# Attention of a fused attention and expert kernel: heads in groups of four instead of two, the softmax sums of the first block as matrix products

## The chip, the core and the metric

The kernel runs on one core of a Trainium2 chip. Four engines of that core matter here: TensorE (PE in the rows; PEld is its weight load), VectorE (DVE), ScalarE (ACT) and GpSimd (POOL), each with an instruction queue that it works through in order; SP issues most DMAs. Matrix products end in PSUM, eight banks of 512 fp32 columns on 128 partitions; everything else lives in SBUF. The metric is the device time in microseconds (us), the median of the runs shown.

## The reference, cut to what matters

```python
def _attn_ref(q, k, v, cap):                 # q, k, v: 4 x 12 x 448 x 64
    scores = scale * np.matmul(q, k.transpose(0, 1, 3, 2))
    scores = cap * np.tanh(scores / cap)     # cap = 30
    scores = scores - np.max(scores, axis=-1, keepdims=True)
    attn = np.exp(scores)
    attn = attn / (np.sum(attn, axis=-1, keepdims=True) + 1e-09)
    return np.matmul(attn, v)
def _moe_ref(x, w_in, w_out, s, b):          # x: 1792 x 768, d_ff 2048
    r = np.maximum(x @ w_in, 0.0)
    return (s * (r * r) + b) @ w_out
def _moe2_ref(x, phi, w1, w2):               # 8 experts with 4 slots each
    logits = x @ phi
    d = softmax of the logits over tokens; slot_input = d.T @ x
    slot_out = relu(slot_input @ w1) @ w2    # per expert
    return (softmax of the logits over slots) @ slot_out
```

The attention's output (12 heads of 64, side by side) is `x` of the second function, whose result is `x` of the third.

## The kernel before

The four batch entries are four blocks of 448 tokens. A block's attention covers 12 heads, taken in six pairs; its result `x` (768 rows of features on six times 128 partitions, 448 tokens wide, kept as a rounded part and a remainder) is the moving operand of the hidden layer (`hidden`, L373), 16 column groups of 18 products `hp` each.

A pair's attention goes in `STEPS` = 8 steps of the generator `attention` (L188). Its 448 keys are four chunks of 112. At steps 0, 2, 4 and 6 `scores` (L104) makes one chunk for both heads: six products `sc` (heads on the two halves of the array's rows; three products each, since q and k are split into a rounded part and a remainder by `prep_pair`, L95), then a tanh on ScalarE into the tile `e`; after the second and the fourth chunk `expo` (L140) takes the exponential of two chunks at once. At steps 5 and 7 `add` (L150) sums the exponentials over the chunks on VectorE into `es`. At step 3 of the next pair `weighted` (L159) finishes the pair: `Sm` is the sum of `es` over its partitions (a product with a column block of ones, 64 wide per head, L169), `U` the weighted values (L172, four chunks, 64 columns per head, two heads side by side in one bank), `rec` the reciprocal of `Sm` on VectorE (L176), `u` = `U` times `rec` (L178), and `split` (L72) writes the rounded part of `u` and the remainder into `x`. `split` rounds on VectorE for the first six pairs (`CASTS`) and on ScalarE for the rest; the remainder is VectorE's always. An fp32 product of the program is two MATMUL rows in the trace, so `U` of a pair is 16 rows and `Sm` 4.

`run` (L551) strings this together. First comes a stage without a hidden layer, here called the first stage: 52 steps of attention, which are block 0's six pairs and four steps of the next pair, with a unit of weight conversion (`convert`, L216: the weights arrive as 64-bit floats, and ScalarE and VectorE make fp32 of them) after every sixth step. Then `block` (L600) runs the hidden layer of block 0, 1 and 2 (here the first three blocks), with the attention of the following block spread over its 48 steps, with conversions in the first two, and with `post` (L405), which turns the hidden layer's result by products `tp` and forms logits `L` and slot sums `pt`. Block 3 has no attention beside it; the tail multiplies by the expert weights.

PSUM is full in the first stage: `psa` holds two banks for `sc`, one for `U`, one for `Sm`; a second pool two more for `sc`; one bank `L` and one bank `T` are kept for `post` and for all small products (`bank`, L69: `tp`, `tw`, `pf`, `pp` and others take turns in the one bank). A scheduler of the framework places each engine's instructions in the order in which it expects them to become ready, so the order in a queue is not that of the code.

## Time and profile before

| | us |
|---|---|
| runs | 681.8, 684.83, 683.8 |
| median of the runs | 683.8 |
| span of the profiled execution, first to last instruction | 677.3 |
| first stage (to the first `hp` product) | 76.4 |
| block 0 with the attention of block 1 | 138.5 |
| block 1 with the attention of block 2 | 137.8 |
| block 2 with the attention of block 3 | 123.1 |
| block 3 and the tail | 201.5 |

The profiled execution is shown by its span; the median of the runs lies 6.5 us above it, which is what lies around the first and the last instruction. The stages are cut at the first `hp` product of each block. The columns PE, DVE and ACT of a view of stretches are busy times; a PE that is busy all the time is an engine with a queue, not an engine at its peak.

### The profile page before, as it was taken

How to read it: one execution, taken by the hardware profiler on the slowest of the kernel's cores; microseconds unless marked ns; L12 is line 12 of the kernel's file. 1: busy time of each engine (PE TensorE's matmuls, PEld its weight loads, DVE VectorE, ACT ScalarE, POOL GpSimd, SP SyncE). 2: the span in 40 equal slices, each digit the busy share in tenths (PEclk: the TensorE clock that was granted, in tenths of full speed). 3: DMA queues.
4: the chain of work that ended last, by engine and by line, in shares of the span. 5: the costliest groups of instructions: out<-in, count | busy, mean ns of one | idle time of the engine just before them, and what ended most of it. 6: DMA issues, size and time to landing. Idle time of an engine off the chain costs nothing.

```text
span 677.3 us, 10643 instructions
## 1 busy us (share of the span) xinstructions
PE 626.0 (92%) x4234; PEld 403.8 (60%) x4234; DVE 386.0 (57%) x574; ACT 416.2 (61%) x688; POOL 4.0 (1%) x11
## 2 busy tenths in 40 slices
...
GB/s 230 195 101 144 153 246 289 219 271 280 172 276 198 215 98 107 51 94 80 74 99 74 75 91 72 46 47 47 370 269 282 274 92 337 420 419 417 418 412 309
DMA packets 43720, 136.55 MB, mean 202 GB/s; under 512 B 4352, under 2 KB 21264, under 8 KB 36752
## 3 DMA queue, kind: packets, MB, share of 16 engines
...
q8 instruction: 35, 0.57, 0.4%
...
## 4 chain that ended last, share of the span: by engine, by line
PE 69%; DMA 14%; DVE 10%; ACT 4%; issue 2%; SPq 0%; DVEq 0%
PE hp L385 32%; DMA wt<-in_w_dram 11%; PE U L172 10%; PE sc L112 8%; PE tp L400 4%; PE Sm L169 3%; DVE rec L176 2%; PE pt L474 2%; PE L L414 2%; PE tw L334 2%; DVE es L157 2%; DVE o L264 1%; ACT e L148 1%; PE si_ps L658 1%; PE idle L502 1%
## 5 line engine op out<-in xcount | busy, mean ns | idle before, releaser
L385 PE MATMUL hp<-x,ws 128*128 128x448 f32 x1152 | 278.1, 380 | 0.0
L385 PEld LDWEIGHTS hp<-x,ws 128*128 128x128 f32 x1152 | 204.3, 188 | 54.3 <-issue 40.5
L370 DVE TENSOR_TENSOR ws<-wr,ws 128x384 fp32r<-128x384 f32 x128 | 70.3, 554 | 99.7 <-ACT ws L369 96.7
L115 ACT ACTIVATE e<-sc,c_tsc 112x896 f32<-112x896 f32 x96 | 96.2, 1010 | 22.5 <-PE sc L112 22.1
L172 PE MATMUL U<-e,v 112*64 112x448 f32 x384 | 88.1, 552 | 9.9 <-DVE u L178 6.8
L369 ACT CAST ws<-wr 128x384 fp32r<-128x384 f32 x128 | 65.1, 514 | 37.8 <-PE hp L385 37.6
L148 ACT ACTIVATE e<-e,c_acap 112x1792 f32<-112x1792 f32 x48 | 86.2, 1797 | 0.4
L176 DVE RECIPROCAL rec<-Sm 128x448 f32<-128x448 f32 x24 | 70.9, 2954 | 16.3 <-PE Sm L169 15.3
L172 PEld LDWEIGHTS U<-e,v 112*64 112x64 f32 x384 | 29.5, 138 | 56.2 <-issue 48.3
L157 DVE TENSOR_TENSOR es<-es,e 112x896 f32<-112x896 f32 x48 | 52.2, 1087 | 18.3 <-ACT e L148 18.1
L402 ACT COPY g<-tp 112x256 f32<-112x256 f32 x128 | 42.0, 376 | 20.4 <-PE tp L400 19.7
L112 PE MATMUL sc<-qh,kh 64*112 64x448 f32 x192 | 46.0, 461 | 8.7 <-DVE kh L73 6.5
L390 ACT ACTIVATE r<-hp 128x448 f32<-128x448 f32 x64 | 34.6, 541 | 25.6 <-PE hp L385 25.4
L112 PEld LDWEIGHTS sc<-qh,kh 64*112 64x112 f32 x192 | 17.8, 176 | 44.2 <-issue 21.0
L400 PE MATMUL tp<-c_cst,r 128*112 128x128 f32 x256 | 38.9, 275 | 1.4 <-ACT r L391 1.2
L112 PE MATMUL sc<-ql,kh 64*112 64x448 f32 x192 | 39.5, 382 | 0.0
L722 ACT COPY wt<-op 128x512 f32<-128x512 f32 x12 | 7.0, 586 | 52.7 <-PE op L717 52.7
L112 PE MATMUL sc<-qh,kl 64*112 64x448 f32 x192 | 39.1, 381 | 0.4 <-DVE kl L74 0.4
L701 PE MATMUL so_ps<-wt,free 128*32 128x128 f32 x768 | 29.8, 303 | 10.0 <-DMA wt<-in_w_dram 10.0
L391 ACT ACTIVATE r<-r 128x448 f32<-128x448 f32 x64 | 37.3, 584 | 0.4
L400 PEld LDWEIGHTS tp<-c_cst,r 128*112 128x112 f32 x256 | 29.5, 133 | 10.5 <-ACT g L402 2.2
L701 PEld LDWEIGHTS so_ps<-wt,free 128*32 128x32 f32 x768 | 24.7, 122 | 14.1 <-DMA wt<-in_w_dram 12.7
...
## 6 DMA issues: line engine op xcount, KB each, us to landing
...
```

Of the source, the lines that this page charges most:

```text
L112: nc.tensor.matmul(sc[:, i, :S], k[r, c * CP:(c + 1) * CP], q[r, :], start=(j == 0), stop=(j == 2))
L115: nc.scalar.activation(self.e[p][-1][:, :, c % 2, :], sc[:, :, :S], AF.Tanh, scale=self.c["tsc"][:CP])
L148: self.nc.scalar.activation(e, e, AF.Exp, scale=self.c["acap"][:CP])
L157: nc.vector.tensor_add(es, es, e[:, :, k, :])
L172: nc.tensor.matmul(U[64 * i:64 * i + 64, :S], v[:, i, k * D:(k + 1) * D], self.chunk(2 * p + i, k), start=(k == 0), stop=(k == NCH - 1))
L176: nc.vector.reciprocal(rec, Sm[:, :S])
L369: self.nc.scalar.copy(hi, u)
L370: self.nc.vector.tensor_sub(lo, u, hi.bitcast(F32))
L385: nc.tensor.matmul(hp[:, :S], ws[kc // 3][:, w, kc % 3, :], x[:, s, kc, :], start=(k == 0), stop=(k == 3 * KC - 1))
L400: self.nc.tensor.transpose(tp[:CP, q * P:(q + 1) * P], r2[:, q * CP:(q + 1) * CP], self.c["idn"])
L402: self.nc.scalar.copy(self.g[q][:CP, :, fc * P:(fc + 1) * P], tp[:CP, 2 * q * P:2 * (q + 1) * P].rearrange("p (a b) -> p a b", b=P))
L701: nc.tensor.matmul(so_ps[32 * e:32 * e + 32, G, :], ht[G][:, f, 32 * e:32 * e + 32], w2[e // 2][:, e % 2, f, :], start=(f == 0), stop=(f = ...
```

## The change

Attention goes in groups of four heads (a quad, two pairs; `Q` in the code), three to a block, 16 steps each. The exponentials of a chunk for four heads are one tile `e` (112 x 4 x 448), as large as two chunks of a pair were, and `expo` works on one such tile after every second scores step. `U` takes two PSUM banks: the four heads stand on four groups of 32 partitions, the first 32 features in one bank and the last 32 in the other, and is made in two portions: chunks 0 and 1 at step 9, chunks 2 and 3 at step 3 of the next quad. `Sm` has 32 partitions per head, so that one bank and one reciprocal serve four heads, spread over both banks of `U` by a broadcast. `u` is written back into `U`'s banks, its rounded part is always made on ScalarE. For the first block (`DIRECT` = `NQ`) `add` is not called: `Sm` gets products of ones with all four chunks, and one with `es`, whose only non-zero row is the small constant; it lives in the bank `L`, which `post` doesn't need yet. Later quads sum over chunks on VectorE as before (three adds of 112 x 1792), `Sm` is taken from the shared bank `T`, and ScalarE copies it to SBUF, where the reciprocal is taken. `es` is filled by GpSimd. The rounding of q and k of pair 1 goes to ScalarE; `qh`, `ql`, `kh`, `kl` get three buffers. The rows of `w_in` are put into the new order of features on the host.

```diff
+NQ = H // 4
...
-DIRECT = 0
+DIRECT = NQ
...
-    def split(self, hi, lo, src, p):
-        (self.nc.vector.tensor_copy if p < CASTS else self.nc.scalar.copy)(hi, src)
+    def split(self, hi, lo, src, vector):
+        (self.nc.vector.tensor_copy if vector else self.nc.scalar.copy)(hi, src)
         self.nc.vector.tensor_sub(lo, src, hi.bitcast(F32))
     def turns(self, tag, i, kept, more, last, shape, dt):
@@ -81,42 +82,46 @@
     def load_pair(self, p):
         if p >= B * NP or p in self.qk:
             return
-        nc, io = self.nc, self.io
         if p < 2:
-            q2, k2 = self.c["early"][p]
-        else:
-            q2 = self.ap.tile([P, S], F32, tag="q2", bufs=1, name="q2")
-            k2 = self.ap.tile([P, S], F32, tag="k2", bufs=1, name="k2")
-            load_qk(nc, io, p, q2, k2)
-        v = self.ap.tile([CP, 2, NCH * D], F32, tag="v", bufs=3, name="v")
-        nc.sync.dma_start(v, io["v"][2 * p:2 * p + 2].rearrange("i p d -> p i d"))
-        self.qk[p] = (q2, k2, v)
+            self.qk[p] = self.c["early"][p]
+            return
+        self.qk[p] = [self.ap.tile([P, S], F32, tag=n, bufs=1, name=n) for n in ("q2", "k2")]
+        load_qk(self.nc, self.io, p, *self.qk[p])
+    def load_v(self, p):
+        if p >= B * NP or p in self.v:
+            return
+        self.v[p] = self.ap.tile([CP, 2, NCH * D], F32, tag="v", bufs=3, name="v")
+        self.nc.sync.dma_start(self.v[p], self.io["v"][2 * p:2 * p + 2].rearrange("i p d -> p i d"))
     def prep_pair(self, p):
         if p >= B * NP:
             return
-        q2, k2, v = self.qk[p]
-        t = [self.ap.tile([P, S], F32R, tag=n, bufs=2, name=n) for n in ("qh", "ql", "kh", "kl")]
-        self.split(t[0], t[1], q2, p)
-        self.split(t[2], t[3], k2, p)
-        self.qk[p] = (*t, v)
+        q2, k2 = self.qk[p]
+        t = [self.ap.tile([P, S], F32R, tag=n, bufs=2 if self.general else 3, name=n) for n in ("qh", "ql", "kh", "kl")]
+        self.split(t[0], t[1], q2, p < CASTS and p != 1)
+        self.split(t[2], t[3], k2, p < CASTS and p != 1)
+        self.qk[p] = t
     def scores(self, p, c):
         nc = self.nc
-        qh, ql, kh, kl, _ = self.qk[p]
-        sc = (self.ps2 if self.ps2 is not None and c % 2 else self.psa).tile([CP, 2, 512], F32, tag="sc", bufs=1, name="sc")
-        for j, (k, q) in enumerate(((kh, qh), (kh, ql), (kl, qh))):
+        Q, j = divmod(p, 2)
+        qh, ql, kh, kl = self.qk[p]
+        sc = (self.ps2 if self.ps2 is not None and j else self.psa).tile([CP, 2, 512], F32, tag="sc", bufs=1, name="sc")
+        for n, (k, q) in enumerate(((kh, qh), (kh, ql), (kl, qh))):
             for i in range(2):
                 r = slice(64 * i, 64 * i + 64)
-                nc.tensor.matmul(sc[:, i, :S], k[r, c * CP:(c + 1) * CP], q[r, :], start=(j == 0), stop=(j == 2))
-        if c % 2 == 0:
-            self.e.setdefault(p, []).append(self.ap.tile([CP, 2, 2, S], F32, tag="e", bufs=3, name="e"))
-        nc.scalar.activation(self.e[p][-1][:, :, c % 2, :], sc[:, :, :S], AF.Tanh, scale=self.c["tsc"][:CP])
+                nc.tensor.matmul(sc[:, i, :S], k[r, c * CP:(c + 1) * CP], q[r, :], start=(n == 0), stop=(n == 2))
+        if j == 0:
+            self.e.setdefault(Q, []).append(self.ap.tile([CP, 4, S], F32, tag="e", bufs=4 if self.general else 3, name="e"))
+        nc.scalar.activation(self.e[Q][c][:, 2 * j:2 * j + 2, :], sc[:, :, :S], AF.Tanh, scale=self.c["tsc"][:CP])
+        if c == NCH - 1:
+            del self.qk[p]
     def chunk(self, g, c):
-        return self.e[g // 2][c // 2][:, g % 2, c % 2, :]
+        return self.e[g // 4][c][:, g % 4, :]
...
-    def expo(self, p, c):
-        ready = [] if c % 2 == 0 else self.e[p][c // 2:]
+    def expo(self, Q, c):
+        ready = self.e[Q][c:c + 1]
         if self.general:
-            ready = self.e[p] if c == NCH - 1 else []
-            for i in range(2 if ready else 0):
-                self.greatest(2 * p + i)
+            ready = self.e[Q] if c == NCH - 1 else []
+            for i in range(4 if ready else 0):
+                self.greatest(4 * Q + i)
         for e in ready:
             self.nc.scalar.activation(e, e, AF.Exp, scale=self.c["acap"][:CP])
-    def add(self, p, half):
-        nc, es, e = self.nc, self.es[:CP], self.e[p][half]
-        if half == 0:
-            nc.vector.tensor_add(es, e[:, :, 0, :], e[:, :, 1, :])
+    def add(self, Q, c):
+        es, e = self.es[:CP], self.e[Q]
+        self.nc.vector.tensor_add(es, e[0] if c == 1 else es, e[c])
+    def sums(self, Q, chunks):
+        nc, c = self.nc, self.c
+        direct = Q < DIRECT
+        if chunks[0] == 0 or not direct:
+            self.Sm = self.psl.tile([P, 512], F32, tag="L", bufs=1, name="Sm") if direct else self.bank("Sm")
+        for k in chunks if direct else ():
+            for i in range(4):
+                nc.tensor.matmul(self.Sm[32 * i:32 * i + 32, :S], c["ones"][:CP, :32], self.chunk(4 * Q + i, k), start=(k == 0), stop=False)
+        if chunks[-1] != NCH - 1:
+            return
+        for i in range(4):
+            nc.tensor.matmul(self.Sm[32 * i:32 * i + 32, :S], c["ones"][:CP + 1, :32], self.es[:CP + 1, i, :], start=not direct, stop=True)
+        rec = self.ap.tile([P, S], F32, tag="rec", bufs=1, name="rec")
+        if Q < NQ:
+            nc.vector.reciprocal(rec, self.Sm[:, :S])
         else:
-            for k in range(2):
-                nc.vector.tensor_add(es, es, e[:, :, k, :])
-    def weighted(self, p):
-        nc, c = self.nc, self.c
-        U = self.psa.tile([P, 512], F32, tag="U", bufs=1, name="U")
-        Sm = self.psa.tile([P, 512], F32, tag="S", bufs=1, name="Sm")
-        v = self.qk[p][-1]
-        for k in (3, 2, 1, 0) if p < DIRECT else ():
-            for i in range(2):
-                nc.tensor.matmul(Sm[64 * i:64 * i + 64, :S], c["ones"][:CP, :64], self.chunk(2 * p + i, k), start=(k == 3), stop=False)
-        for i in range(2):
-            nc.tensor.matmul(Sm[64 * i:64 * i + 64, :S], c["ones"][:CP + 1, :64], self.es[:CP + 1, i, :], start=(p >= DIRECT), stop=True)
-        for k in range(NCH):
-            for i in range(2):
-                nc.tensor.matmul(U[64 * i:64 * i + 64, :S], v[:, i, k * D:(k + 1) * D], self.chunk(2 * p + i, k),
-                                 start=(k == 0), stop=(k == NCH - 1))
-        del self.qk[p], self.e[p]
-        rec = self.ap.tile([P, S], F32, tag="rec", bufs=1, name="rec")
-        nc.vector.reciprocal(rec, Sm[:, :S])
-        u = self.ap.tile([P, S], F32, tag="u", bufs=1, name="u")
-        nc.vector.tensor_mul(u, U[:, :S], rec)
-        xt = self.xtile(p // NP)
-        self.split(xt[:, 0, p % NP, :], xt[:, 1, p % NP, :], u, p)
+            nc.scalar.copy(rec, self.Sm[:, :S])
+            nc.vector.reciprocal(rec, rec)
+        self.rec = rec
+    def weighted(self, Q, chunks):
+        nc = self.nc
+        if chunks[0] == 0:
+            self.U = self.psa.tile([P, 2, 512], F32, tag="U", bufs=1, name="U")
+        for k in chunks:
+            for h in range(2):
+                for i in range(4):
+                    nc.tensor.matmul(self.U[32 * i:32 * i + 32, h, :S], self.v[2 * Q + i // 2][:, i % 2, k * D + 32 * h:k * D + 32 * h + 32],
+                                     self.chunk(4 * Q + i, k), start=(k == 0), stop=(k == NCH - 1))
+    def finish(self, Q):
+        nc = self.nc
+        xt = self.xtile(Q // NQ)
+        k = 2 * (Q % NQ)
+        hi, lo = (xt[:, s, k:k + 2, :] for s in range(2))
+        u = self.U[:, :, :S]
+        nc.vector.tensor_mul(u, u, self.rec[:, None, :].to_broadcast([P, 2, S]))
+        self.split(hi, lo, u, False)
+        del self.e[Q], self.v[2 * Q], self.v[2 * Q + 1]
...
     def attention(self):
-        for p in range(2):
-            self.load_pair(p)
+        self.load_pair(0)
+        self.load_pair(1)
+        self.load_v(0)
         self.prep_pair(0)
-        self.es = self.ap.tile([P, 2, S], F32, name="es")
-        self.nc.vector.memset(self.es, EPS)
+        self.prep_pair(1)
+        self.load_v(1)
+        self.es = self.ap.tile([P, 4, S], F32, name="es")
+        self.nc.gpsimd.memset(self.es, EPS)
         if not self.general:
-            self.nc.vector.tensor_scalar(self.es, self.es, self.c["eps"], None, op0=ALU.mult)
-        self.nc.vector.memset(self.es[:CP], 0.0)
-        last = B * NP
-        for p in range(last + 1):
-            for k in range(STEPS):
-                if p < last and k % 2 == 0:
-                    if k == 0:
-                        self.load_pair(p + 1)
-                    self.scores(p, k // 2)
-                    self.expo(p, k // 2)
-                elif k == 3 and p:
-                    self.weighted(p - 1)
-                elif k in (5, 7) and p < last:
-                    if p >= DIRECT and (k == 7 or not self.general):
-                        for h in range(2) if self.general else (k // 7,):
-                            self.add(p, h)
-                    if k == 5:
-                        self.prep_pair(p + 1)
+            self.nc.gpsimd.tensor_scalar(self.es, self.es, self.c["eps"], None, op0=ALU.mult)
+        if DIRECT:
+            self.nc.gpsimd.memset(self.es[:CP], 0.0)
+        last = B * NQ
+        for Q in range(last + 1):
+            for s in range(2 * STEPS):
+                if Q < last:
+                    if s % 2 == 0:
+                        c, j = divmod(s // 2, 2)
+                        self.scores(2 * Q + j, c)
+                        if j:
+                            self.expo(Q, c)
+                    self.between(Q, s)
+                if not self.general and Q and s in (1, 3) and not (s == 1 and Q - 1 < DIRECT):
+                    if s == 1:
+                        self.add(Q - 1, 3)
+                    else:
+                        self.sums(Q - 1, (2, 3))
+                        self.weighted(Q - 1, (2, 3))
+                        self.finish(Q - 1)
                 yield
+    def between(self, Q, s):
+        if s == 0:
+            self.load_pair(2 * Q + 2)
+        if s == 4:
+            self.load_v(2 * Q + 1)
+            self.load_v(2 * Q + 2)
+        if s == (13 if self.general else 7):
+            self.prep_pair(2 * Q + 2)
+            self.load_pair(2 * Q + 3)
+        if s == 15:
+            self.prep_pair(2 * Q + 3)
+        if self.general:
+            if s == 14:
+                for k in range(1, NCH) if Q >= DIRECT else ():
+                    self.add(Q, k)
+                self.sums(Q, range(NCH))
+                self.weighted(Q, range(NCH))
+                self.finish(Q)
+        else:
+            if s == 9:
+                if Q < DIRECT:
+                    self.sums(Q, (0, 1))
+                self.weighted(Q, (0, 1))
+            if s in (9, 13) and Q >= DIRECT:
+                self.add(Q, 1 if s == 9 else 2)
...
+    wi = wi.reshape(NQ, 4, 2, D // 2, FF).transpose(0, 2, 1, 3, 4)
```

On TensorE near the end of the first stage, before (the sums `Sm` of a pair are 2 products, `U` 8):

```order
L169 MATMUL Sm<-es,c_ones 64x448 x2
L112 MATMUL sc<-qh,kh 112x448 x2
L112 MATMUL sc<-ql,kh 112x448 x2
L112 MATMUL sc<-qh,kl 112x448 x2
L112 MATMUL sc<-qh,kh 112x448 x2
L112 MATMUL sc<-ql,kh 112x448 x2
L112 MATMUL sc<-qh,kl 112x448 x2
L112 MATMUL sc<-qh,kh 112x448 x2
L112 MATMUL sc<-ql,kh 112x448 x2
L112 MATMUL sc<-qh,kl 112x448 x2
L316 MATMUL pp<-o,c_misc 32x256 x4
L172 MATMUL U<-e,v 64x448 x5
```

and now, on TensorE at the end of the second quad and the start of the third:

```order
L115 MATMUL sc<-qh,kh 112x448 x2
L115 MATMUL sc<-ql,kh 112x448 x2
L115 MATMUL sc<-qh,kl 112x448 x2
L168 MATMUL Sm<-e,c_ones 32x448 x8
L172 MATMUL Sm<-es,c_ones 32x448 x4
L189 MATMUL U<-e,v 32x448 x16
L115 MATMUL sc<-qh,kh 112x448 x2
L115 MATMUL sc<-ql,kh 112x448 x2
L115 MATMUL sc<-qh,kl 112x448 x2
```

Where two products of sums and at most eight of `U` stood between scores, 28 products of sums and weighted values now stand in a row.

On TensorE in block 2, before, one pair:

```order
L385 MATMUL hp<-x_2235,ws 128x448 x6
L169 MATMUL Sm<-es,c_ones 64x448 x2
L172 MATMUL U<-e,v 64x448 x8
L385 MATMUL hp<-x_2235,ws 128x448 x6
L112 MATMUL sc<-qh,kh 112x448 x2
```

and now, on TensorE in block 2, a quad's sums with the later portion of its `U`:

```order
L438 MATMUL hp<-x_2484,ws 128x448 x6
L172 MATMUL Sm<-es,c_ones 32x448 x4
L189 MATMUL U<-e,v 32x448 x16
L438 MATMUL hp<-x_2484,ws 128x448 x6
L453 MATMUL tp<-c_cst,r_3844 112x128 x4
```

The group comes once for four heads; the earlier portion, another 16 products of `U`, stands by itself, without sums, elsewhere in the row.

On VectorE in block 0, where `rec` is of the first quad beside the hidden layer, before:

```order
L176 RECIPROCAL rec<-Sm 128x448
L238 TENSOR_SCALAR o<-o 128x768
L178 TENSOR_TENSOR u<-U,rec 128x448
L260 SCALAR_TENSOR_TENSOR o<-raw,o 128x768
L370 TENSOR_TENSOR ws<-wr,ws 128x384
L264 SCALAR_TENSOR_TENSOR o<-raw,o 128x768
L74 TENSOR_TENSOR x_894<-u,x_894 128x448
```

and now, on VectorE:

```order
L158 TENSOR_TENSOR es<-e 112x1792
L178 RECIPROCAL rec<-rec 128x448
L378 COPY c_hh<-pf 128x64
L199 TENSOR_TENSOR U<-U,rec 128x2x448
L291 TENSOR_SCALAR wr<-wr 128x768
L423 TENSOR_TENSOR ws<-wr,ws 128x384
L313 SCALAR_TENSOR_TENSOR wr<-raw,wr 128x768
L75 TENSOR_TENSOR x_1151<-U,x_1151 128x896
```

The chain has the same links, twice as wide behind the reciprocal, and the next quad's first add now stands ahead of the reciprocal.

## Rows read from the trace of the kernel before

**Rows 1.** The page's part 1: engine, busy us, share of the span, instructions

```profile
span 677.3 us, 10643 instructions
PE 626.0 (92%) x4234; PEld 403.8 (60%) x4234; DVE 386.0 (57%) x574; ACT 416.2 (61%) x688; POOL 4.0 (1%) x11
```

**Rows 2.** Busy time of each engine by stretch (columns in the first row)

```profile
core 0: us, PE busy (x) PEld busy (x) DVE busy (x) ACT busy (x) POOL busy (x), PEclk, DMA share, GB/s
20.00:75.00 55.00, 44.50 (x241) 18.36 (x237) 53.92 (x67) 44.60 (x43) 0.00 (x0) 0.94 0.44 141
0.00:76.40 76.40, 56.65 (x293) 24.45 (x293) 69.12 (x95) 56.35 (x55) 2.98 (x9) 0.93 0.51 164
76.40:214.90 138.50, 136.34 (x755) 86.13 (x753) 119.57 (x159) 112.12 (x175) 0.00 (x0) 1.00 0.71 244
...
352.70:475.80 123.10, 123.02 (x688) 79.87 (x687) 68.39 (x93) 86.64 (x148) 0.00 (x0) 1.00 0.23 69
560.00:677.30 117.30, 91.15 (x1250) 59.19 (x1249) 23.51 (x62) 11.87 (x22) 0.54 (x1) 0.86 0.97 390
```

**Rows 3.** VectorE's instructions by line in the first stage: xcount, busy, mean ns, idle

```profile
L176 DVE RECIPROCAL rec<-Sm 128x448 f32<-128x448 f32 x6 | 17.7, 2952 | 0.8 <-PE Sm L169 0.8
L157 DVE TENSOR_TENSOR es<-es,e 112x896 f32<-112x896 f32 x12 | 13.0, 1084 | 0.3 <-ACT e L148 0.3
L154 DVE TENSOR_TENSOR es<-e 112x896 f32<-112x896 f32 x6 | 6.3, 1045 | 0.0
...
L178 DVE TENSOR_TENSOR u<-U,rec 128x448 f32<-128x448 f32 x5 | 3.1, 610 | 0.0
...
L73 DVE CAST x<-u 128x448 fp32r<-128x448 f32 x5 | 1.9, 386 | 0.0
...
L194 DVE MEMSET es<- 128x896 f32 x1 | 0.8, 805 | 0.1
```

**Rows 4.** ScalarE's instructions by line in the first stage

```profile
L115 ACT ACTIVATE e<-sc,c_tsc 112x896 f32<-112x896 f32 x26 | 25.4, 1006 | 12.5 <-PE sc L112 12.2
L148 ACT ACTIVATE e<-e,c_acap 112x1792 f32<-112x1792 f32 x13 | 23.4, 1799 | 0.2
L233 ACT ACTIVATE wr<-raw 128x768 f32<-128x768 f32 x4 | 3.6, 908 | 2.9 <-DMA raw<-in_w_in_dram 2.9
...
L73 ACT CAST qh<-q 128x448 fp32r<-128x448 f32 x2 | 1.1, 571 | 0.0
```

**Rows 5.** Instructions in order of time, TensorE in block 2: start, us, what

```profile
379.34 3.64 PE L474 MATMUL pt<-g,c_tmp 112*32 112x512 f32 x32
382.91 0.46 PE L112 MATMUL sc<-qh,kh 64*112 64x448 f32 x2
...
388.97 0.96 PE L414 MATMUL L<-r,c_hh 128*32 128x448 f32 x8
389.86 0.46 PE L112 MATMUL sc<-qh,kh 64*112 64x448 f32 x2
...
392.51 0.97 PE L169 MATMUL Sm<-es,c_ones 113*64 113x448 f32 x4
393.31 3.18 PE L172 MATMUL U<-e,v 112*64 112x448 f32 x16
396.42 1.50 PE L385 MATMUL hp<-x,ws 128*128 128x448 f32 x6
```

**Rows 6.** The same view, VectorE and ScalarE at the start of the first stage

```profile
4.96 0.39 DVE L73 CAST qh<-c_tmp 128x448 fp32r<-128x448 f32 x1 [0.59 <-DMA c_tmp<-in_qT_dram]
...
7.92 2.13 ACT L115 ACTIVATE e<-sc,c_tsc 112x896 f32<-112x896 f32 x2 [3.80 <-PE sc L112]
```

**Rows 7.** The same view, ScalarE and TensorE at the end of the first stage

```profile
70.68 1.91 ACT L115 ACTIVATE e<-sc,c_tsc 112x896 f32<-112x896 f32 x2
...
72.71 1.83 ACT L148 ACTIVATE e<-e,c_acap 112x1792 f32<-112x1792 f32 x1
...
76.36 1.06 PE L385 MATMUL hp<-x,ws 128*128 128x448 f32 x4
```

2 lines of the change are left out of this document (1 added, 1 removed).

## The prediction

> **What bounds the kernel now.** I read the page's first part, then the stretches, then the groups by line in the first stage, then the order of time where TensorE is full. The page says that TensorE is busy for 92% of 677.3 us [rows 1], but that is a mean over stages with three different limits. The stretches part them [rows 2]. In the first stage VectorE has 69.1 us of 76.4, and between 20 and 75 us it has 53.9 of 55.0, while TensorE has 44.5 and ScalarE 44.6: there VectorE is the limit. In blocks 0 and 2 TensorE has 136.3 of 138.5 and 123.0 of 123.1, always at the full clock: there the end is set by how many matrix rows are issued, and VectorE (119.6 and 68.4) and ScalarE stand beside it; block 1 is of the same kind. From 560 us on the DMA share is 0.97: the tail is a stream of weights that starts with block 3's progress. So time taken off the first stage or off TensorE's rows in blocks 0 to 2 moves the end by as much, since the tail's stream is issued later and moves along; time taken off VectorE counts in the first stage alone.
>
> **The change in blocks 0 to 2** (the attention of blocks 1 to 3: 9 quads, 18 pairs). For a pair, `Sm` goes from 392.51 to 393.31, 0.80 us for 4 rows, and `U` to 396.42, 3.11 us for 16 rows [rows 5]: two heads run side by side, so 2 and 8 rounds of 0.39. Four heads cost 2 x 3.91 = 7.82. After it `Sm` has 8 rows of 32 columns, four side by side. `L` has that very shape: 388.97 to 389.86, 0.89. `U` has two portions of 32 rows, four side by side, 448 columns wide; `pt` is 32 such rows of 512 columns in 3.57 (379.34 to 382.91), and 448/512 of that is 3.12 [rows 5]. Four heads then cost 0.89 + 2 x 3.12 = 7.13 where `Sm` stands alone, and about 7.0 where it stands beside `U` and pays no entry. `U` gains nothing: twice as many rounds, each with twice as many products. What goes is one of two sums. I take 0.75 a quad: 9 x 0.75 = 6.7 us. Against it stand the visits: I counted 336 stretches of one kind of array shape in TensorE's order of the three blocks before and 347 after. `L`'s two rounds at `pt`'s pace (3.57/8 x 448/512 = 0.39) would be 0.78, so a visit costs 0.11 beyond its rounds, and 11 of them 1.2. The blocks give 5.5 us, with bounds of 3.5 (`Sm` never beside `U`, every visit dearer by half) and 8 (no price for visits, 0.82 a quad and a little idle time gone).
>
> VectorE loses there too: 6 adds of 1.05 to 1.08 become 3 twice as wide (1.08 is 0.61 at half the width plus 0.47, so 1792 columns are 2.0 each, 6.0 against 6.4), one of two reciprocals goes (2.95), and two products and two remainders of 0.61 become one each of 1.08 [rows 3]. That is 3.7 us less a quad, hidden behind TensorE and counted at nothing. ScalarE rounds once at 896 columns (about 0.95 against 2 x 0.57, the row of a cast [rows 4]) and copies `Sm` for about 0.55: 0.4 more a quad, in stretches where it has idle time; counted at nothing.
>
> **The change in the first stage.** VectorE loses the 18 adds, 13.0 + 6.3 = 19.3 us; three of six reciprocals, 8.9; the roundings of `x`, 6 x 0.39 = 2.3; the two fills of `es`, 1.6; pair 1's two roundings, 0.8; and 0.9 in the wider products and remainders [rows 3]: 34 of 69 us. It is no limit any more. Next in line are ScalarE and TensorE, which feed each other through two pairs of banks for `sc`.
>
> ScalarE first. Its first tanh starts at 7.92 [rows 6]; that start hangs on q and k of pair 0 and stays. Then come 12 times two tanhs and one exponential. When it runs through, two tanhs take 1.91 and, from 70.68 to 72.71 with a copy between, the pace of the three is about 3.55 with the exponential's overlap [rows 7]: 42.6. Six conversions of 0.9 (0.85 each in a queue) make 5.1, three weight roundings, a little narrower than the cast of 0.57, 1.5, a small copy 0.4 (both estimates from that cast's row), four roundings of q and k 2.0, two of `x` 1.9 [rows 4]: 53.5 in all, so the last exponential of block 0 ends at 61.4 if ScalarE never waits. Behind it TensorE has the last chunk's sums and those of `es`, 16 rows or 4 rounds, 1.5, and a portion of `U`, 3.1: the first `hp` at 66.0.
>
> It will wait, though. TensorE's own work in the stage grows: sums by products are 20 products a quad, 10 rounds of 0.39, 3.9 us, against 2 x 0.8 for two pairs, 7 us over three quads. The order shows where they fall. In the second quad 28 products in a row, 14 rounds, 5.4 us, stand between scores; ScalarE has two ready tanhs and an exponential, 3.6, less what it did while the last scores were made: it waits 1.5 to 2. In the third quad the scores of pair 5 stand behind sums that need the exponential issued just before: 3. The same once in the second quad, half of it hidden: 1. The second quad's `U` needs its banks free, and their remainder stands behind three conversions of 0.95 on VectorE: 0.5. The first weights are now loaded behind three more DMAs: 0.5. And 1 for the start: 0.7 for GpSimd (below), the rest for the slower clock, 0.93 in the mean of the stage [rows 2]. Together 7.7, so the first `hp` at 73.5 to 74, against 76.36 [rows 7]: 2.5 us off. Bounds: 66.0 is a gain of 10.4; with waits twice as long (15.4) the first `hp` comes at 81.4, a loss of 5.
>
> **Sum.** 677.3 - 5.5 - 2.5 = 669.3 for the span. The runs' median lies 6.5 above the span, so 675.8, and I say 676.
>
> **A rule against it.** The fill of `es` moves to GpSimd and is twice as wide. Before, VectorE fills 896 columns in 0.8 [rows 3]; GpSimd shows no fill of such size, so its own pace isn't in the trace. If it keeps VectorE's pace, two fills and a product of 1792 columns are 4.8 us from about 4.3 on (an estimate: just ahead of VectorE's own first instruction of that part), beside VectorE's first roundings, from 4.96 on, which the first scores wait for [rows 6]. If VectorE is held for none of it, nothing is lost; if for all of it, the whole first stage starts 4.8 later: 676 + 4.8 - 0.7 = 680. I take 0.7, the rest of the first fill that overlaps the first rounding. The Trainium skill, page "SBUF — State Buffer", section "Who interferes with whom", says that VectorE and GpSimd share one pair of ports as an exclusive lock, that a copy or cast in a two-port mode can be blocked for the whole of a GpSimd instruction, and that a two-input VectorE operation is blocked by a GpSimd instruction that reads SBUF. No row before shows it, since GpSimd does no such work there; by that rule the case of 680 is the likelier of the two ends.
>
> **The rivals.**
> *ScalarE runs through.* The scheduler's gaps close, the first `hp` comes at 66 to 68, and the blocks give 6: 677.3 - 9 - 6 + 6.5 = 669. For it: 12.2 of the 20 us that ScalarE is idle in the stage end with `sc` [rows 2, 4], which came late because VectorE was behind. Against it: the rows of 28 products.
> *The first stage gives nothing.* TensorE's 7 us more and the waits above, GpSimd's hold included, eat all that VectorE gave; the blocks give 4: 680 to 682. For it: TensorE has 56.7 of 76.4 us already and gets 7 more, in bursts.
> *Slower: the one pair of `U` banks.* Before, `U` is made in one go and a whole pair's time lies before the next. Now the next quad's first portion of `U` must find the banks free 10 to 12 us after `Sm`: by the order, 10.6 us of TensorE's own rows lie between them in the first such quad. In this time run a copy on ScalarE (0.55), the next quad's first add, which stands ahead of the reciprocal (2.0), the reciprocal (2.95), the product (1.08), the rounding (0.95) and the remainder (1.08): 8.6 without a wait in either queue. It decides from 2 us of such waits on. At 4 us of them a quad TensorE stands 2 us nine times, 18 us, and the end is 676 + 18 = 694; at 3 us it is 685. For it: in block 0 VectorE has 119.6 of 138.5 and ScalarE 112.1 [rows 2], so conversions stand in both queues. Against it: VectorE loses 3.7 a quad, and in block 2 it has 68.4 of 123.1.
>
> **How the numbers follow.** Forecast 676 (own range 672 to 680): 0.47. ScalarE runs through, 669: 0.19. First stage gives nothing, 681: 0.15. GpSimd holds VectorE by the rule, 680: 0.05. Slower by the banks, 685 to 694: 0.14. About 0.5%, 3.4 us, is what a measurement of this kernel can tell from no change, so faster means under 680.4 and slower over 687.2. The first two cases and a part of the next two are faster: 0.70. Same: the rest of these and the mildest part of the last: 0.19. Slower: 0.11. The range leaves out the outer half of the case of 669 below its value and the upper part of the last: 666 to 687.
>
> **What the next profile should show.** The three blocks between their first `hp` products: 399.4 us before in sum, about 394 after. `Sm` of a quad in 0.8 to 0.9, a portion of `U` in 3.0 to 3.2; were a portion to take 4, the blocks would lose. VectorE near 36 us of the first stage, ScalarE near 60, and the first `hp` at 73 to 75, with ScalarE's idle time ended by `sc`. TensorE's waits for a remainder of `x` (the line of `split`) before `U`: under 1 us a quad, or the slower rival holds. The first scores within 1 us of where they were. Wrong altogether: a first `hp` after 77, or a sum of the blocks above 400.

## The result: no gain, and where the forecast gain went

The changed kernel takes 686.2 us (median; 683.61 to 691.05) against 682.35 for the kernel before (679.28 to 684.83): a ratio of 1.0063, with a 95% interval of 1.0041 to 1.0085. It is slower by 0.4 to 0.9%, where 1% faster was forecast.

The profiled execution has a span of 685.4. By stage (columns as in [rows 2], cut at the first `hp` of each block and at the last `hp`):

```profile
core 0: us, PE busy (x) PEld busy (x) DVE busy (x) ACT busy (x) POOL busy (x), PEclk, DMA share, GB/s
0.00:76.97 76.97, 60.50 (x488) 24.05 (x489) 47.10 (x61) 60.34 (x62) 11.21 (x12) 1.00 0.57 185
76.97:210.36 133.39, 130.94 (x819) 80.95 (x818) 104.44 (x133) 111.25 (x168) 0.00 (x0) 1.00 0.71 239
210.36:358.76 148.40, 144.43 (x913) 89.44 (x912) 76.36 (x100) 107.12 (x184) 0.60 (x1) 0.99 0.31 99
358.76:481.68 122.92, 122.53 (x783) 79.01 (x782) 59.01 (x75) 86.69 (x147) 0.00 (x0) 1.00 0.21 65
...
559.37:685.45 126.08, 92.07 (x1271) 58.23 (x1270) 24.16 (x63) 14.26 (x27) 0.54 (x1) 0.90 0.95 379
```

Against [rows 2] and the stage times before: the first stage 76.4 to 77.0, block 0 138.5 to 133.4, block 1 137.8 to 148.4, block 2 123.1 to 122.9; the blocks together 399.4 to 404.7. What follows 559 us is a stream of weights (DMA share 0.95); it varies by itself, between 121 and 127 us over all the kernels below, which share its code. Two spans alone would say 8.1 us; the medians say 3.9. The listed time of an execution lies 1.8 to 1.9 above its span (687.23 to 685.4 here), not 6.5: the profiled execution before would be listed at 679.2, 3.1 under its kernel's median. Each kernel has one profile, so a stage that stands against the profile before can look some 3 us worse than it is.

**The head of the first stage.** VectorE, GpSimd and ScalarE in order of time:

```profile
4.99 1.59 POOL L218 MEMSET es<- 128x1792 f32 x1 [0.94 <-DVE c_eps L818]
6.68 5.03 POOL L220 TENSOR_SCALAR es<-es,c_eps 128x1792 f32<-128x1792 f32 x1
...
5.18 1.65 DVE L74 CAST qh<-c_tmp 128x448 fp32r<-128x448 f32 x1 [0.59 <-DMA c_tmp<-in_qT_dram]
...
7.04 3.85 DVE L75 TENSOR_TENSOR ql<-c_tmp,qh 128x448 fp32r<-128x448 f32 x1
10.81 0.61 DVE L75 TENSOR_TENSOR kl<-c_tmp,kh 128x448 fp32r<-128x448 f32 x1
...
12.23 2.13 ACT L118 ACTIVATE e<-sc,c_tsc 112x896 f32<-112x896 f32 x2 [3.80 <-PE sc L115]
```

The cast that took 0.39 [rows 6] takes 1.65 beside GpSimd's fill, the remainder that takes 0.61 one row on takes 3.85 beside GpSimd's product. The first tanh comes at 12.23 instead of 7.92.

**Pieces of `U`.** TensorE in block 1 (first part) and block 2 (second part):

```profile
235.09 1.69 PE L189 MATMUL U<-e,v 112*32 112x448 f32 x10
236.71 0.66 PE L387 MATMUL tw<-c_cst,o 128*128 128x128 f32 x4
237.30 0.96 PE L189 MATMUL U<-e,v 112*32 112x448 f32 x8
238.19 0.65 PE L453 MATMUL tp<-c_cst,r 128*112 128x128 f32 x4
238.77 1.70 PE L189 MATMUL U<-e,v 112*32 112x448 f32 x14
240.40 4.93 PE L438 MATMUL hp<-x,ws 128*128 128x448 f32 x23
...
370.63 0.96 PE L189 MATMUL U<-e,v 112*32 112x448 f32 x8
371.52 0.65 PE L453 MATMUL tp<-c_cst,r 128*112 128x128 f32 x4
372.10 2.46 PE L189 MATMUL U<-e,v 112*32 112x448 f32 x24
374.49 1.50 PE L438 MATMUL hp<-x,ws 128*128 128x448 f32 x6
```

Read from start to next start. A whole portion of 32 rows takes 3.12 to 3.15, as forecast. Cut into 8 and 24 rows it takes 0.89 + 2.39 = 3.28. Cut into 10, 8 and 14 it takes 1.62 + 0.89 + 1.63 = 4.14. The 10 rows are five products of two rows: four run side by side in two rounds of 0.39, and the fifth takes two rounds more by itself. So a piece of `n` products costs ceil(n/4) times two rounds, and only a cut at a multiple of eight rows is nearly free. Counted so from the traces, `U` in blocks 0 to 2 needs 144 rounds whole, has 156 before (pairs: ceil(n/2)) and 166 after. Ten rounds at 0.389 are 3.9 us; `U` grew from 60.6 to 64.6. The Trainium skill, page "TensorEngine Tiling (Array Packing)", section "Key Properties", says that a change of tiling mode drains TensorE. These rows agree: products on either side of a foreign one don't share a round. With `Sm`, whose products have the same shape as theirs, they share one (18 rows ahead of `Sm` take 1.94 in block 1, not 2.33), and the counts here take that for a cut too, so they are right to a few rounds.

**A stall in block 1.** ScalarE and TensorE, and then stretches around it:

```profile
222.38 1.79 ACT L153 ACTIVATE e<-e,c_acap 112x1792 f32<-112x1792 f32 x1
224.07 0.99 ACT L118 ACTIVATE e<-sc,c_tsc 112x896 f32<-112x896 f32 x1
...
222.85 0.67 PE L438 MATMUL hp<-x,ws 128*128 128x448 f32 x2
225.12 0.46 PE L115 MATMUL sc<-qh,kh 64*112 64x448 f32 x2 [1.60 <-ACT e L118]
...
227.08 0.46 PE L115 MATMUL sc<-qh,kh 64*112 64x448 f32 x2 [1.10 <-ACT e L118]
```
```profile
222.00:227.80 5.80, 3.10 (x21) 1.63 (x20) 5.80 (x6) 4.81 (x5) 0.00 (x0) 1.00 0.40 136
227.80:231.30 3.50, 3.50 (x20) 1.94 (x18) 3.33 (x3) 3.15 (x5) 0.00 (x0) 0.51 0.60 202
```

Scores wait for the tanh that frees their banks. That tanh stands behind an exponential of 1.79 us on ScalarE, and TensorE's order has only two rows of `hp` (0.67 us) to do meanwhile. After these 5.8 us with 3.1 busy the granted clock is 0.51, the lower level (1.2 GHz), for 3.5 us. The blocks before had no such stretch.

### The profile page after: what moved, and what is told of

The parts are those of the page before. It is cut to its first block, busy times and chain, and to the rows that moved or that the text cites. A ratio compares the mean times of both kernels' runs of the same rounds, so it can differ in the third digit from the quotient of the medians.

```text
span 685.4 us, 11531 instructions
## 1 busy us (share of the span) xinstructions
PE 628.2 (92%) x4714; PEld 395.7 (58%) x4714; DVE 333.5 (49%) x482; ACT 425.0 (62%) x693; POOL 12.4 (2%) x14
## 4 chain that ended last, share of the span: by engine, by line
PE 71%; DMA 12%; ACT 9%; DVE 3%; issue 2%; SPq 0%; DVEq 0%; ACTq 0%
PE hp L438 32%; PE U L189 10%; DMA wt<-in_w_dram 9%; PE sc L115 8%; PE tp L453 4%; ACT e L118 3%; ACT e L153 3%; DMA raw<-in_w_outT_dram 3%; PE hps L732 2%; PE pt L527 2%; PE L L467 2%; PE tw L387 2%; PE pp L369 1%; PE Sm L172 1%; PE si_ps L711 1%
## 5 line engine op out<-in xcount | busy, mean ns | idle before, releaser
L118 ACT ACTIVATE e<-sc,c_tsc 112x896 f32<-112x896 f32 x96 | 95.9, 1008 | 18.3 <-PE sc L115 17.7
L189 PE MATMUL U<-e,v 112*32 112x448 f32 x768 | 91.0, 542 | 0.2 <-DVE x L75 0.2
L189 PEld LDWEIGHTS U<-e,v 112*32 112x32 f32 x768 | 25.0, 109 | 44.9 <-issue 42.7
L158 DVE TENSOR_TENSOR es<-es,e 112x1792 f32<-112x1792 f32 x18 | 36.4, 2023 | 23.7 <-ACT e L153 23.7
L115 PEld LDWEIGHTS sc<-qh,kh 64*112 64x112 f32 x192 | 18.2, 174 | 46.2 <-issue 22.1
L115 PE MATMUL sc<-ql,kh 64*112 64x448 f32 x192 | 41.5, 384 | 3.2 <-DVE ql L75 3.2
L115 PE MATMUL sc<-qh,kl 64*112 64x448 f32 x192 | 40.8, 379 | 0.0
L178 DVE RECIPROCAL rec<-rec 128x448 f32<-128x448 f32 x9 | 26.6, 2951 | 24.5 <-ACT rec L177 24.5
L453 PEld LDWEIGHTS tp<-c_cst,r 128*112 128x112 f32 x256 | 29.4, 133 | 11.9 <-ACT g L455 2.4
```

The lines of the kernel that those rows point to most:

```text
L115: nc.tensor.matmul(sc[:, i, :S], k[r, c * CP:(c + 1) * CP], q[r, :], start=(n == 0), stop=(n == 2))
L118: nc.scalar.activation(self.e[Q][c][:, 2 * j:2 * j + 2, :], sc[:, :, :S], AF.Tanh, scale=self.c["tsc"][:CP])
L158: self.nc.vector.tensor_add(es, e[0] if c == 1 else es, e[c])
L189: nc.tensor.matmul(self.U[32 * i:32 * i + 32, h, :S], self.v[2 * Q + i // 2][:, i % 2, k * D + 32 * h:k * D + 32 * h + 32], self.chunk(4 * ...
L453: self.nc.tensor.transpose(tp[:CP, q * P:(q + 1) * P], r2[:, q * CP:(q + 1) * CP], self.c["idn"])
```

## The account of blocks 0 to 2

TensorE's time by tile, each product from its start to the next start without gaps over 50 ns, worked out from the traces:

| us | before | after |
|---|---|---|
| `Sm` | 14.7 | 7.4 |
| `U` | 60.6 | 64.6 |
| `sc` | 59.8 | 61.7 |
| `hp` | 198.2 | 199.6 |
| `tw`, `tp`, `pp` | 37.0 | 39.4 |
| other tiles | 25.9 | 25.3 |
| gaps | 3.2 | 6.7 |
| sum | 399.4 | 404.7 |

`Sm` gave 7.3, more than the 6.7 forecast. It was given back as 4.0 of unfilled rounds of `U`, 3.5 of gaps, and 5.7 in `sc`, `hp`, `tw`, `tp` and `pp` (0.6 less in other tiles), of which the half clock is 3.5/2 = 1.75. For the other 4.0 of these no run shows a cause. The blocks can't be read one by one, since the `Sm` of one quad has moved from block 0 to block 1 (16, 32 and 24 rows).

The experiments in one table ("first `hp`", blocks and gaps from each profiled execution, rounds counted from it; the time is the median, the ratio is against the kernel before on the same chip, with its 95% interval):

| kernel | first `hp` | block 0, 1, 2 | gaps in them | `U` rounds | time | ratio |
|---|---|---|---|---|---|---|
| before | 76.4 | 138.5, 137.8, 123.1 | 3.2 | 156 | 682.4 | |
| after | 77.0 | 133.4, 148.4, 122.9 | 6.7 | 166 | 686.2 | 1.0063 (1.0041 to 1.0085) |
| e1 fill on VectorE | 74.3 | 134.7, 148.4, 122.9 | 7.1 | 166 | 682.6 | 1.0029 (1.0004 to 1.0053) |
| e2 e1, adds | 71.8 | 134.4, 150.6, 122.9 | 9.1 | 166 | 683.9 | 1.0019 (0.9998 to 1.0041) |
| e3 e1, first block rounds on VectorE | 74.0 | 135.6, 149.4, 122.9 | 7.8 | 166 | 685.3 | 1.0036 (1.0004 to 1.0068) |
| e4 before, products of ones | 86.1 | 138.2, 142.6, 123.1 | 2.0 | 162 | 695.8 | 1.0185 (1.0151 to 1.0219) |
| e5 e1, `U` whole | 75.6 | 133.9, 144.0, 126.1 | 7.0 | 144 | 681.6 | 0.9992 (0.9967 to 1.0017) |
| e6 e2, `U` whole | 74.2 | 143.9, 144.3, 126.1 | 11.9 | 144 | 691.1 | 1.0116 (1.0082 to 1.0149) |
| e7 before, `U`, `Sm` whole | 78.1 | 140.8, 146.9, 126.2 | 4.9 | 144 | 692.8 | 1.0147 (1.0121 to 1.0172) |
| e8 e1, `U` cut more | 75.9 | 149.5, 160.2, 136.7 | 12.0 | 218 | 726.2 | 1.0629 (1.0584 to 1.0675) |
| e9 e1, blocks as written | 78.2 | 195.9, 154.6, 129.6 | 80.0 | 146 | 761.0 | 1.1132 (1.1084 to 1.118) |
| e10 before, blocks as written | 80.5 | 192.5, 152.4, 126.8 | 68.6 | 144 | 756.0 | 1.109 (1.1051 to 1.1129) |
| e13 e5, later finish | 79.9 | 140.1, 143.4, 121.5 | 15.0 | 144 | 686.6 | 1.0066 (1.0038 to 1.0093) |
| e14 e1, all rounding on VectorE | 74.1 | 142.1, 152.1, 122.7 | 13.3 | 166 | 692.9 | 1.0135 (1.0094 to 1.0176) |
| e16 e1, block 1's `U` whole | 74.5 | 134.7, 141.0, 122.8 | 6.3 | 154 | 677.2 | 0.9934 (0.9909 to 0.996) |
| e17 e2, block 1's `U` whole | 70.7 | 134.7, 148.2, 122.8 | 11.7 | 152 | 678.2 | 0.9963 (0.9945 to 0.9982) |
| e18 before, fill on GpSimd | 74.4 | 141.0, 142.9, 123.1 | 3.3 | 156 | 681.3 | 0.9995 (0.9972 to 1.0019) |

The gaps aren't all that waits cost. The kernel before, e4, e7, e16 and e18 have no time at the lower clock in the blocks; the changed kernel and e1 have 3.4 us, e5 6.8, e13 and e17 10.2, e8 13.6, e14 20.5. In e5 it falls on `U` itself (the first 32 rows below, and 48 rows at 176.6 that take 6.23 instead of 4.65):

```profile
224.76 4.88 PE L190 MATMUL U<-e,v 112*32 112x448 f32 x32
...
216.00:224.80 8.80, 6.35 (x37) 4.15 (x38) 8.80 (x10) 7.64 (x9) 0.00 (x0) 1.00 0.13 44
224.80:229.50 4.70, 4.70 (x38) 1.34 (x40) 3.13 (x3) 0.00 (x0) 0.00 (x0) 0.64 0.85 293
```

After 8.8 us with 6.35 busy the clock is 0.64 in the mean, and the portion takes 4.70 to the next start instead of 3.14.

## Experiments on the first stage

**e1, the fill back on VectorE.**

```diff
-        self.nc.gpsimd.memset(self.es, EPS)
+        self.nc.vector.memset(self.es, EPS)      # and the two that follow it
```

> The changed kernel with the three instructions that fill `es` back on VectorE, at the same width of 1792 columns; nothing else. Theory H (GpSimd's fill holds VectorE): the first tanh starts at 7.9 to 8.5 instead of 12.23, the first `hp` comes 3 to 4.3 us earlier, at 72.7 to 74.0, the time falls to about 682 to 683 (ratio 0.999 to 1.001 to the kernel before). Rival T (TensorE and ScalarE pace the first stage and the late start is hidden): the first `hp` stays within 1 us of 76.97 and the time at 686. Either way the three blocks between their first `hp` keep their 404.7 within 3 us if their loss has nothing to do with the head.

```profile
6.06 0.62 DVE L75 TENSOR_TENSOR ql<-c_tmp,qh 128x448 fp32r<-128x448 f32 x1
...
10.01 1.15 DVE L220 TENSOR_SCALAR es<-es,c_eps 128x1792 f32<-128x1792 f32 x1
...
8.25 1.00 ACT L118 ACTIVATE e<-sc,c_tsc 112x896 f32<-112x896 f32 x1
11.15 1.01 ACT L118 ACTIVATE e<-sc,c_tsc 112x896 f32<-112x896 f32 x1 [1.90 <-PE sc L115]
```

The remainder takes 0.62 again, the first tanh starts at 8.25, and the first `hp` comes 2.6 us earlier (3 to 4.3 were expected); the second tanh still waits, since VectorE's own fill (1.55) stands ahead of pair 1's remainders. Theory H holds, a little under its size. The blocks keep their loss (406.0).

**e18, the fill on GpSimd in the kernel before.** The three instructions go from `nc.vector` to `nc.gpsimd`, nothing else.

> The kernel before with nothing changed but the three instructions that fill `es`, on GpSimd at their old width of 896 columns. Theory H (while GpSimd works on SBUF, VectorE's casts and two-input operations beside it don't finish): at half of the changed kernel's widths GpSimd's fills take about 0.8 and its product 2.5 us, the cast or the remainder beside them grows by up to 2.5 us, and the first tanh starts 2 to 2.5 us later, at 10 to 10.5. Rival (what was late in the changed kernel was VectorE's order or the load of k and q, not GpSimd): casts 0.39, remainders 0.62, the first tanh at 7.9 to 8.4.

```profile
5.79 2.75 POOL L196 TENSOR_SCALAR es<-es,c_eps 128x896 f32<-128x896 f32 x1
...
5.04 0.90 DVE L73 CAST qh<-c_tmp 128x448 fp32r<-128x448 f32 x1 [0.59 <-DMA c_tmp<-in_qT_dram]
...
6.16 1.34 DVE L74 TENSOR_TENSOR ql<-c_tmp,qh 128x448 fp32r<-128x448 f32 x1
7.42 0.61 DVE L74 TENSOR_TENSOR kl<-c_tmp,kh 128x448 fp32r<-128x448 f32 x1
```

The hold is there (0.90 and 1.34 instead of 0.39 and 0.62) but smaller: the first tanh comes 0.9 later, at 8.85. A remainder at 7.42 runs at full pace although the product's row lasts to 8.54, so by these rows, rough as GpSimd's are, VectorE isn't held for the whole of GpSimd's row (in the changed kernel the remainder at 10.81 is such a case too). The next two casts, beside the second fill, take 0.84 and 1.11. The stage ends 2.0 us earlier all the same, for VectorE, its limit, has less to do. And blocks 0 and 1, in which nothing was changed, take 283.9 instead of 276.3 in the profiles: the scheduler had placed their products anew, in 392 stretches of one tile instead of 376. The medians don't show all of this: they are equal (0.9995), so with the stage 2.0 shorter some 2 of the 7.6 us are left (an estimate from these two numbers); the profile before lies 3.1 under its kernel's median, this one (683.96) 2.7 above.

**e2, adds instead of products of ones** (`DIRECT = 0` on e1), **and e4, products of ones in pairs** (`DIRECT = NP` on the kernel before).

> The changed kernel with the fill of `es` on VectorE and, in the first block too, adds over the chunks on VectorE instead of products of ones; the quads stay. Theory D (the products of ones relieve VectorE, which is the limit of that stage): three quads get 3 adds of 2.0 us on VectorE, 18 us, and TensorE loses 96 rows of `Sm`, 10 us; the first `hp` comes later than with the products, by 3 to 8 us (76 to 81), the time 686 to 690. Rival T (TensorE's bursts of 28 products are what ScalarE waits for): the first `hp` comes earlier, by 2 to 4 us, and the time is 679 to 681.

> The kernel before, in pairs of heads, with one part of the change alone: in the first block the sums over the chunks are products of ones (16 more rows a pair), without VectorE's 18 adds. Theory D (VectorE is the limit of that stage): VectorE loses 19.3 of 69.1 us, TensorE gains 6 x 16 rows at 0.2, 19 us, on 56.7: TensorE is then at 76 and becomes the limit, so the first `hp` moves by no more than 3 us either way, 74 to 79, and the time is 681 to 686. If the quads are what makes the sums by products pay (32 columns a head, four side by side: 10 instead of 19 us of TensorE), this kernel is slower in the first stage than the changed kernel with the fill on VectorE, by 1 to 5 us. The blocks stay at 399.4 within 1.5.

e2: the first `hp` comes 2.5 us earlier without the products of ones. VectorE has 60.1 us of the 71.8: three reciprocals less and the moved roundings relieve it enough to make the adds too. The rival was right on the stage, not on the time, since block 1 took 2.2 more. e4: 9.7 us later, far outside what was expected: 96 more rows of `Sm` two side by side take 18.3 us of TensorE. In quads the same sums take 10.6. So the direct sums are a cost in the first stage in either form, and it is the quads that relieve VectorE.

**e3, the first block's rounding of `x` on VectorE** (`split(hi, lo, u, Q < NQ)` on e1).

> The changed kernel with the fill on VectorE and with the rounding of `x` of the first block back on VectorE (three casts of 128 x 896, 0.95 each on ScalarE). Theory A (ScalarE has become the limit of the first stage): ScalarE is 2.8 us lighter there, and the first `hp` comes 1.5 to 2.8 us before that of the kernel with the fill alone. Rival (both wait on TensorE's order): within 0.7 us.

0.4 us earlier: the rival. ScalarE's 2.8 us there were hidden.

## Experiments on the blocks

**e5, e6, e7: precedence for `U`.**

```diff
+        with self.tc.high_priority():
             for k in chunks:
                 for h in range(2):
                     for i in range(4):
                         nc.tensor.matmul(self.U[...
```

> The changed kernel with the fill of `es` on VectorE and with the products of `U` given precedence in the scheduler, so that they stand in stretches of 8, 16 or 24 products (8 or more side by side in fours) instead of pieces like 5, 4, 7 or 1, 15. Theory R (four products run side by side, a piece takes a whole number of rounds of two times 0.389 us, whatever it has in it): `U` in blocks 0 to 2 goes from 164 rounds to 144, 63.8 to 56 us; the three blocks fall from 405.9 to about 398 and the time from 682.6 to 674 to 676 (ratio 0.988 to 0.991). Rival V (what costs is the change of array shape, 0.11 each, not the unfilled round): 11 changes more, so no gain, 682 to 684. Rival S (block 1 loses by ScalarE being late, not by `U`): block 1 stays at 147 to 149 and the blocks gain no more than 3 us.

> The same as the kernel with whole stretches of `U`, and in the first block adds on VectorE instead of the products of ones. Theory: the first `hp` comes 2 to 3 us before that of the other kernel (as 71.8 against 74.3 with cut stretches), and the time is 672 to 675, the shortest of all so far. Rival: with whole stretches of `U` TensorE is no limit in the first stage, and the adds win nothing there: both times within 1 us.

> The kernel before, in pairs of heads, with the same precedence for `Sm` and `U`, so that all their stretches have an even number of products. Theory R: `U` and `Sm` in blocks 0 to 2 go from 154 and 46 rounds to 144 and 36, at 0.389 that is 5 to 8 us less in stretches, most of it in block 0; the time is 676 to 680. If pairs gain as much as quads by whole stretches, the quads are worth only their `Sm`: this kernel stands 3 to 6 us above the quads with whole stretches. Rival V: 42 changes of shape more at 0.11 take the gain back, 682 to 684.

In e5 `U` is whole, 144 rounds, and takes 60.9 instead of 64.6; block 1 gains 4.4. At 0.389 the 22 rounds less should be 8.6: two portions at the lower clock take 3.1 of the difference, and pieces of 16 rows, at 1.64 instead of 1.56, most of the rest. Block 2 loses 3.2, since now `U` cuts the scores (block 2 of e5):

```profile
389.10 0.46 PE L115 MATMUL sc<-qh,kh 64*112 64x448 f32 x2
389.40 0.36 PE L115 MATMUL sc<-ql,kh 64*112 64x448 f32 x1
389.68 1.71 PE L190 MATMUL U<-e,v 112*32 112x448 f32 x16
391.33 0.45 PE L115 MATMUL sc<-ql,kh 64*112 64x448 f32 x1
391.33 0.65 PE L115 MATMUL sc<-qh,kl 64*112 64x448 f32 x2
```

A set of six takes 0.79 to 0.80 whole; here it is 3 and 3, 0.59 each. `sc` in the blocks goes from 62.3 to 66.3 (e7: from 59.8 to 69.7, and e7 is slower for it). Theory R's rounds came out, and its time (674 to 676) did not: it left out the clock and who pays next. e6 adds gaps (20.3 us in the first stage, 7.7 in block 0; e5 has 13.8 and 2.3) and ends at 691.1 where 672 to 675 was expected.

**e8, more cuts** (`high_priority(offset=100)`).

> The changed kernel with the fill on VectorE and with a smaller precedence for the products of `U`, which cuts them more than without: 76 pieces in blocks 0 to 2 (33 without, 27 in whole stretches), 216 rounds instead of 164 and 144. Theory R: `U` there takes 216 x 0.389 = 84 us, 20 more than without, and the three blocks about 20 us more, 426, the time about 702. Rival V (0.11 a change of shape): 83 changes more, 9 us, the time about 692.

```profile
411.36 0.94 PE L190 MATMUL U<-e,v 112*32 112x448 f32 x2
412.23 0.40 PE L516 MATMUL et_ps<-c_cst,c_tmp 32*112 32x32 f32 x4
412.56 0.96 PE L190 MATMUL U<-e,v 112*32 112x448 f32 x8
```

Two rows, one product, take 0.87; eight rows take no longer (0.78 to 0.89 to the next start). `U` takes 90.5 for 218 rounds (64.6 for 166): 52 rounds are 20.2. Of the other 5.7 about 2 are rows at the lower clock (a portion of 32 rows takes 4.08 at 188.6), and 43 more pieces make the rest, under 0.1 each. With 3.7 more on `sc`, 6.5 on `hp` and 4.9 of gaps the blocks lose 40 against e1: both theories were under it, V (0.11 a change alone) by far.

**e9 to e12: TensorE's order as the code is written** (`tc.manual_schedule` for TensorE around blocks 0 to 2: e9 on e1, e10 on the kernel before, e11 on e2; in e12 around the first stage as well).

> The changed kernel with the fill of `es` on VectorE, and in blocks 0 to 2 TensorE's products stand in the order in which the code is written, so the scheduler cuts no stretch: `U` in 18 stretches of 16 products (144 rounds instead of 164), 317 changes of array shape instead of 373. Theory R (what the cuts cost: unfilled rounds of 0.389 and about 0.11 per stretch): 20 rounds, 7.8 us, and 56 stretches, 6.2 us, go: the blocks fall from 405.9 to about 392 and the time to about 669. Rival W (an order as written makes TensorE wait for ScalarE's exponentials and VectorE's remainders): idle time of TensorE in the blocks rises above 14 us and the time is 682 or more.

> The kernel before, in pairs of heads, with TensorE's products of blocks 0 to 2 in the order in which the code is written: `U` and `Sm` 144 and 36 rounds (150 and 42 in the scheduler's order), 329 changes of shape (371). Theory R: 12 rounds, 4.7 us, and 42 stretches, 4.6 us, go: blocks 399.4 to about 390, time about 673. The quads in the same kind of order then stand 8 us below in the blocks: 18 rounds of `Sm`, 7.0, and 12 stretches, 1.3; that was the 5.5 of the prediction without the scheduler's cuts. If quads and pairs come out within 2 us of each other in the blocks, it isn't the cuts that ate the gain of the quads. Rival W as with the quads: waits above 9 us.

> As the quads in the order as written, and the first block's sums by adds on VectorE instead of products of ones. Theory: TensorE's order in the blocks is the same, so the blocks are within 2 us of those; the first `hp` comes at 71 to 73 instead of 74.3, since TensorE loses 96 rows of `Sm`: the time is 1.5 to 3 us below the other. Rival: 0 or above it.

> As the quads with adds and blocks as written, and the first stage's products as written too: `U` there 48 rounds instead of 56. Theory R: 8 rounds, 3.1 us, less of TensorE in the first stage; the first `hp` 1 to 3 us earlier, 69 to 71. Rival W: in the first stage scores stand behind `U` that waits for exponentials, ScalarE runs dry, and the first `hp` comes at 74 to 80.

Rival W in all four. What TensorE waited for in e9, from 70 to 490 us (total, times, longest):

```profile
PE pp L369 <- DVE o L317: 47.7, 6, 13.1
PE Sm L172 <- ACT g L455: 9.3, 5, 1.9
```

Products of the weight conversion wait in line for VectorE, and `Sm`, which in quads shares the bank `T`, for that bank's last reader. e11 takes 757.6 us and e12 773.1 (first `hp` at 93.3). Block 2, which has no conversions, can be compared: without gaps 122.1 for quads and 124.4 for pairs. That 2.3 is about what three quads save by `Sm` (3 x 0.75); with gaps (7.5 and 2.4) pairs win by 2.8.

**e13, e14, e15: a later finish, and ScalarE relieved.** e13 is e5 with the second half of a quad at steps 4 and 6 instead of 1 and 3; e14 is e1 with `split(hi, lo, u, True)`; e15 is both.

> The changed kernel with the fill on VectorE, precedence for the products of `U`, and the second half of a quad three steps later (add at step 4, sums, `U` and the finish at step 6; 55 instead of 52 steps in the first stage). Counted from the order with prices from the traces (a round of `U` or `Sm` 0.389 twice, a started pair of `sc` products 0.195, a stretch of `sc` 0.2 and of `hp` 0.11 beside its products of 0.2185): TensorE's work in blocks 0 to 2 is 388 us, against 398 with the fill alone and 395 with precedence alone, since neither `U` nor most of `sc` is cut. Theory R (the count of rounds and stretches is what the blocks cost, with some 7 us of waits and slower clock on top): the blocks take 395 to 397 and the time is 672 to 675. Rival W (the waits grow, since `U` and the third tile `e` are held longer): idle time of TensorE in the blocks above 12 us, the time 680 or more.

> The changed kernel with the fill on VectorE, and the rounding of `x` on VectorE for all blocks; the counted work of TensorE in the blocks is the same (398). Theory A (in block 1 TensorE waits because ScalarE is late: 0.95 more per quad for the rounding and 0.55 for the copy of `Sm`): TensorE's 3.9 us of idle time in block 1 and the stretch at half clock go, block 1 falls from 148.4 to 143 to 145, the time to 677 to 679. Rival: idle time in block 1 stays at 3 us or above, the time within 1.5 us of 682.6.

> Precedence for `U`, the later finish, and the rounding of `x` on VectorE. Theory R: counted work of the blocks 387.6, so the time within 1 us of the kernel with the later finish alone, 671 to 675. Theory A: 1 to 3 us below it, since ScalarE, the engine that releases `sc`, has 0.95 less a quad. Rival: 2 or more above it, since the rounding waits in VectorE's queue behind conversions and holds the banks of `U`.

In e13 neither `U` nor most of `sc` is cut, and TensorE's time without gaps falls from 398.8 to 390.0, about as counted (1.8 of it are scores that the three more steps put into the first stage). The gaps rise from 7.1 to 15.0 and eat it (scores wait 5.3 for their tanhs, block 0's first products 3.0 for the last `x`, others 3.9 for the weights' remainder), and two portions of `U` run at the lower clock (48 rows in 6.29 and 6.37 instead of 4.65). e14 refutes theory A: with less on ScalarE block 1 takes 152.1, its gaps are 6.4, scores still wait 3.9 for tanhs, TensorE waits 2.7 for a rounding that stands in VectorE's queue, and 13.7 us of the block are at the lower clock. e15 takes 687.0 us (ratio 1.0059, 1.0036 to 1.0081), the same as e13.

**e16 and e17: `U` whole in block 1 alone** (precedence only for `5 <= Q < 9`, on e1 and on e2).

> The changed kernel with the fill on VectorE, and precedence for the products of `U` only in the quads whose `U` falls into block 1 (and the last one before). Counted work of TensorE in the blocks: 395 us (398 with the fill alone, 395 with precedence everywhere), with the first stage and block 2 left as with the fill alone. Theory R with the waits unchanged: first `hp` at 74.3, block 1 from 148.4 to 144 to 145, block 2 at 122.9, the time 677 to 679, 0.992 to 0.995 of the kernel before. Rival (any change of the order makes other waits, and these are of the size of the gain): idle time of TensorE in the blocks above 9 us, the time 681 to 685.

> The same with adds on VectorE instead of products of ones in the first block: counted work 394. Theory R: first `hp` at 71.8, block 0 at 134.4, block 1 at 145 to 147 instead of 150.6, block 2 at 122.9: the time 677 to 680. Rival: idle time in the blocks above 11 us (9.1 without precedence), 682 to 686.

```profile
209.14:350.11 140.97, 138.34 (x906) 86.24 (x905) 74.06 (x97) 105.71 (x182) 0.54 (x1) 1.00 0.33 105
```
```profile
224.94 4.72 PE L190 MATMUL U<-e,v 112*32 112x448 f32 x48
```

e16 does what theory R said, and more: 12 rounds less, block 1 from 148.4 to 141.0 (144 to 145 were expected), no half clock, and 677.2 us, faster than both kernels. The first stage and blocks 0 and 2 stay within 0.2 us of e1, so the gain is block 1's. Of its 7.4 us, 4.6 are the rounds (`U` from 23.4 to 18.8), 1.3 the gaps and 1.7 the half clock, and other pieces cost 0.2 more; the stall is shorter, with 1.4 of waits for tanhs instead of 2.7. Rounds and stall changed in one edit, so no run shows what the rounds would have given alone. In e17 the first `hp` comes another 3.7 earlier, but block 1 has 8.3 of gaps (5.1 of it one wait of `hp` for a rounding of `x`) and 10.2 us at the lower clock, where 48 rows of `U` take 7.25: the stage's gain doesn't reach the end. Its idle time (11.7) is the rival's and its time (678.2) the theory's. It is faster than the kernel before too, and not than e16.

## Why the prediction was wrong, step by step

- The measured 686.2 lies at the upper end of the stated range (666 to 687), beside the rival of the `U` banks (685 to 694), and that is luck: in the blocks TensorE waited for no remainder of `x` before `U`. The gain that was forecast isn't there, and the prediction's own sign of being wrong, blocks above 400, came (404.7).
- `Sm` of a quad in 0.78 to 0.89 and 6.7 us saved: right (7.3).
- "`U` gains nothing: twice as many rounds, each with twice as many products": the step that failed. It priced whole portions. The scheduler cuts them, and with four products to a round a cut leaves up to three places empty where pairs leave one: 4.0 us lost. The order was at hand and showed stretches such as 5, 4, 7 and 1, 15.
- "11 of them 1.2", the price of the visits: in the traces there are 4 changes of shape more (333 to 337; by tile the number falls, 376 to 371). Their number isn't the price; where they cut is. `sc`, `tw` and the rest cost 5.7 more, the half clock included.
- Gaps in the blocks were taken as unchanged; they rose by 3.5, with a tanh late for the one pair of banks of `sc`. Why ScalarE was late there isn't settled: relieving it (e14) made it worse. The stretch at the lower clock behind the stall (1.75) was not in the sum at all.
- First stage: without GpSimd's fill the first `hp` comes at 74.3, against 73.5 to 74 forecast; VectorE has 46.2 there (36 forecast, without the fills, which are 4.3), ScalarE 60.0 (60). The size held; that the direct sums bring it was wrong (e2).
- The fill was priced at 0.7 and cost 2.6 at the first `hp` (e1), 4.0 at the first tanh. Its own pace, too, was underrated: GpSimd fills 1792 columns in 1.59, about as VectorE (1.55), but takes 5.03 for the product that VectorE does in 1.15. The rule set beside it in the prediction ("SBUF — State Buffer" of the Trainium skill, "Who interferes with whom") had the contention right, though in e18 the hold is shorter than GpSimd's whole row: the case deserved far more than 5%.
- Sum: 2.5 + 5.5 us of gain became 0.6 + 5.3 of loss in the traces, 3.9 in the medians. By the ratios the fill makes about 2.3 us of it (1.0063 to 1.0029, intervals that overlap), and whole portions of `U` in block 1, with the stall and the clock that changed with them, are worth 6.5 (1.0029 to 0.9934), more than all the rest.
